# Routing the first 27 chunks of an attention and expert kernel in three groups of nine, in seven pieces, behind the value products

## The chip, the cores and the metric

The kernel runs on one core of a Trainium2 chip. The metric is device time in microseconds (us). The core has TensorE (PE, and PEld for its weight loads), VectorE (DVE), ScalarE (ACT), GpSimd (POOL) and SyncE (SP, which issues most DMAs). Each engine works through its own instructions in program order and waits on semaphores for the others.

## The reference

A windowed causal attention over 8 batches, 8 heads, 576 rows and 64 columns a head, whose output of 4608 tokens by 512 columns goes into a mixture of 8 experts; each token goes to the one expert with the largest logit.

```python
scores = scale * np.matmul(q, k.transpose(0, 1, 3, 2))
mask = (rel >= 0) & (rel < window)                     # window = 128
scores = np.where(mask, scores + bias[None], -1000000000.0)
scores = scores - np.max(scores, axis=-1, keepdims=True)
attn = np.exp(scores)
attn = attn / (np.sum(attn, axis=-1, keepdims=True) + 1e-09)
x = np.matmul(attn, v)                                 # to (4608, 512)
logits = x @ w_gate
expert_idx = np.argmax(logits, axis=1)
for e in range(E):
    mask = expert_idx == e
    h = np.maximum(x[mask] @ w1[e], 0.0)
    out[mask] = gate_w[mask, None] * (h @ w2[e])
```

## The kernel before

The tokens are worked through in 36 chunks of 128 rows. Chunk `ch` is spread over the steps from `4*ch` on, and the work of several chunks is interleaved: a function `step(s)` issues, for step `s`, whatever the table `LAGS` has due there. Up to step 151 (`HAND = 152`) every engine keeps exactly this order. The steps of a chunk are four, and a step's number modulo 4 tells what it issues:

- **0**: the first scores of a chunk (the heads' first half: TensorE L129 and L138 into `s_ps`), the first transposes of the chunk before (L168, `pe` into `t_ps`, copied by ScalarE to `pT`, L170), and the weighing of the new scores: on VectorE a masked copy (L147 or L152) and the maximum `nmax` (L155), on ScalarE four exponentials (L159).
- **1**: `rows` of an older chunk: the row products (L206, into the bank `r_ps`), then on VectorE the reciprocal (L203), the scaling `x_sb` from `r_ps` (L211) and the logits `lg` (L1145); then the second transposes (L168).
- **2**: the second scores and their weighing, as in step 0.
- **3**: the value products of an older chunk (L196, 32 matmuls for most chunks, 16 for the first chunk of a batch; one chunk in nine, which holds the last 64 rows of two batches, has them in two halves).

There are two `s_ps` banks, one `t_ps` and one `r_ps`. A new `r_ps` can be written once everything that touched the old one is done.

**Routing.** When the logits of a group of chunks are there, `route` finds each token's expert and its place in that expert's list. It is a generator: at each `yield` it stops, and `step` resumes it at the end of a later step. The groups are in `GROUPS` as (first chunk, number of chunks G). Its pieces before are five: (1) from `mx` (L404) to `prev` (L417), on VectorE, with one exponential `ex` on ScalarE; (2) the rank products on TensorE (L421, L422, L425: G+1 matmuls) into spare columns of the current `r_ps`, then on VectorE `pick` (L427), which reads them, and eight short instructions up to `t` (L438; a ninth, `s_cnt`, where a group ends with chunk 26), with the gates' DMAs on SP's queue (L496); (3) `p`, `lp` (L448, 128 columns a chunk), `c`, `big`; (4) `c`, `c`, `eq` (L458, 48 columns a chunk) and the two `rr` (L462); (5) the index products on TensorE (L468, 2G matmuls) into the spare columns of the then current `r_ps`, and their sum into `base` on VectorE (L470). For the group that ends with chunk 26, piece 3 also holds `shift_late` (one matmul L478 and five VectorE instructions from L480 on), whose result the chunks from 27 on need.

A group without an entry in `PACE` has one piece in each step of one kind (`s % 4`); a group with an entry (by its first chunk) has its pieces in the steps that the entry lists. The group (30, 5) is routed from step 149 on and finished in `route_last`, which also routes chunk 35. At step 134 the first lists are read (`e_idx`), and rows are gathered for the first expert. From step 58 to 113 each chunk also has ScalarE and GpSimd split a half of a weight tile (`wh` L924, `wl` L929).

After the attention the experts' two layers run, weights streamed, with TensorE as the engine that everything else feeds.

Of the kernel before, what the change touches and what calls it, by code (L numbers as in the profile page):

```python
# [10 lines left out]
F32 = mybir.dt.float32  # L11
F32R = mybir.dt.float32r
BF16 = mybir.dt.bfloat16
# [8 lines left out]
N, DM, E, F = B * S, H * D, 8, 1024  # L22
# [14 lines left out]
def attention(ctx, tc, st, qT, kT, v, c1, cb, iw, load_c2, chunk_done, chunks, begun):  # L37
# [48 lines left out]
    def warm_up(n):  # L86
        w_ps = ps_x.tile([128, 512], F32, name="x_ps")
        for _ in range(n):
            keep(tc, nc.tensor.matmul(out=w_ps, lhsT=warm[:, 0:128], rhs=warm, start=True, stop=True))

    def early(op):
        bank = ps_s.tile([128, 2, 2, 256], F32, name="s_ps")[:, 0] if op not in "zg" else None
        st["early"][0](op, bank if bank is None else bank.rearrange("p a b -> p (a b)"))
# [124 lines left out]
    for ch, subs in enumerate(chunks):  # L218
        for b, i in subs:
            k = (b, i // 4)  # L220
# [48 lines left out]
    def step(s):  # L269
        st["step"] = s  # L270
        if s == 0:
            begun(0)
        if s == 12:
            begun(1)
        for f, b, m in ahead.get(s, ()):
            f(b, m)
        for k, ch in sorted(plan.get(s, ()), key=lambda x: (1.5 if x[0] == 9 else x[0], x[1])):
            do(k, ch)
        if s < len(WU) - 1:
            warm_up(WU[s + 1])  # L280
        for k in list(st["stages"]):
            if k[1] <= s and (s in PACE[k[2]] if k[2] in PACE else s % 4 == 2):
                k[1] = s + 1
                if next(k[0], k) is k:
                    st["stages"].remove(k)
        n, i = divmod(s - FETCH, 8)
        if 0 <= n < 7 and i in (0, 1, 4, 5):
            (st["round"], st["rest_of"])[i % 4](n, i // 4)
        if (s - FETCH + 12) % 8 == 0 and 0 <= (s - FETCH + 12) // 8 < 8:
            st["load"]((s - FETCH + 12) // 8)  # L290
        if s in EP:
            early(EP[s])

    with tc.manual_schedule(engines=HANDS(nc)):
        HELD[0] = True
        for s in range(HAND):
            step(s)
        HELD[0] = False
    for s in range(HAND, max(plan) + 1):
        step(s)  # L300
# [29 lines left out]
TT = 6  # L330
# [5 lines left out]
LW = (0, 0, 0, 0)  # L336
FREE_T = 146
WU = (9, 1, 1, 1, 1, 1, 2, 2, 2, 2, 2, 1, 0)
PACE = {21: (122, 126, 130, 132, 134), 27: (138, 142, 144, 146, 148), 30: (149, 150)}
GROUPS = ((0, 5), (5, 5), (10, 5), (15, 6), (21, 6), (27, 3), (30, 5), (35, 1))  # L340
EARLY = 256
LATE = 27
NE = 7
# [51 lines left out]
def route(tc, st, lg, c0, G, groups):  # L395
    nc = tc.nc
    rp = st["rp"]
# [3 lines left out]
    sc3 = [128, G, E * TT]  # L401
    sp3 = [128, G, 128]
# [31 lines left out]
    s = st["rank"][:, c0:c0 + G]  # L434
# [8 lines left out]
    if c0 + G == LATE:  # L443
        shift_late(tc, st, cnt)
    p = rp.tile([128, G], F32, name="p")
    nc.vector.scalar_tensor_tensor(out=p, in0=t, scalar=-128.0, in1=s, op0=ALU.mult, op1=ALU.add)
    lp = rp.tile(sp3, BF16, name="lp")
    nc.vector.tensor_tensor(out=lp, in0=st["i128"].unsqueeze(1).to_broadcast(sp3),  # L448
                            in1=p.unsqueeze(2).to_broadcast(sp3), op=ALU.is_equal)
    c = rp.tile([128, G], F32, name="c")  # L450
    nc.vector.tensor_scalar(out=c, in0=mk, scalar1=-float(TT), scalar2=float(TT * E), op0=ALU.mult, op1=ALU.add)
    big = rp.tile([128, G], F32, name="big")
    nc.vector.tensor_scalar(out=big, in0=s, scalar1=128 * TT - 0.5, scalar2=1000.0, op0=ALU.is_ge, op1=ALU.mult)
    yield
    nc.vector.tensor_tensor(out=c, in0=c, in1=t, op=ALU.add)
    nc.vector.tensor_tensor(out=c, in0=c, in1=big, op=ALU.add)
    eq = rp.tile(sc3, F32, name="eq")
    nc.vector.tensor_tensor(out=eq, in0=st["i128"][:, 0:E * TT].unsqueeze(1).to_broadcast(sc3),  # L458
                            in1=c.unsqueeze(2).to_broadcast(sc3), op=ALU.is_equal)
    rr = rp.tile([128, G, 2, E * TT], BF16, name="rr")  # L460
    for k, n in enumerate(("tokh", "tokl")):
        nc.vector.tensor_tensor(out=rr[:, :, k, :], in0=eq,  # L462
                                in1=st[n][:, c0:c0 + G].unsqueeze(2).to_broadcast(sc3), op=ALU.mult)
    yield
# [34 lines left out]
def route_last(tc, st, lg, ch, groups):  # L499
    nc = tc.nc  # L500
    rp = st["rp"]
# [19 lines left out]
    nc.tensor.matmul(out=rank, lhsT=tri[:, 0, :], rhs=oh, start=True, stop=False)  # L521
    nc.tensor.matmul(out=rank, lhsT=tri[:, 1, :], rhs=prev, start=False, stop=True)
    for r in st["rest"]:
        next(r)
        next(r)
    st["warm"](1)
    rr = rp.tile([128, 2, E], BF16, name="l_rr", bufs=1)
    for k, n in enumerate(("tokh", "tokl")):
# [2 lines left out]
    s = st["rank"][:, ch:ch + 1]  # L531
# [8 lines left out]
    for t in range(t0, TT):  # L540
        lp = rp.tile([128, 128], BF16, name=f"l_lp{t}", bufs=1)
# [577 lines left out]
def attn_moe_kernel(ctx, tc, qT, kT, v, c1, cb, c2, iw, w12, out):  # L1119
# [9 lines left out]
    with ExitStack() as actx:  # L1129
# [9 lines left out]
        def done(ch, subs, x_sb):  # L1139
            c0, G = next((c, n) for c, n in GROUPS if c <= ch < c + n)  # L1140
            g = ch - c0
# [12 lines left out]
            if g == G - 1:  # L1154
# [16 lines left out]
                else:  # L1171
                    r = route(tc, st, lg, c0, G, groups)
                    st["stages"].append([r, st["step"] + (c0 not in PACE), c0])

# [46 lines left out]
```

## Time and profile before

| | us |
|---|---|
| median of 3 runs | 672.38 (671.96 to 673.99) |
| the profiled execution | 670.84, with a span of 669.1 |
| TensorE busy | 645.0 |
| VectorE busy | 397.8 |
| ScalarE busy | 315.3 |
| GpSimd busy | 311.7 |

The span runs from the first to the last instruction; the 1.7 us between it and the execution's own time lie around it. Busy times are sums over the span; waits are told by the instruction that came last before the waiting one could start. The attention with its routing takes roughly the first 235 us of the span, the experts the rest. TensorE's granted clock is 1.00 in nearly the whole span.

### The profile page before, as it was taken

To read this page: it belongs to the slowest core of one execution; us is meant where nothing else is said; L and a number is where in the kernel's file an instruction comes from. 1 tells how busy PE (TensorE), PEld (TensorE's weight loads), DVE (VectorE), ACT (ScalarE), POOL (GpSimd) and SP (SyncE) were. 2 spreads that over 40 slices of the span, in tenths; PEclk is the share of its full clock that TensorE was granted. 3 is DMA by queue.
4 is the path that set the end of the run, shared out by engine and by line. 5 is a ranking of instruction groups with operands and counts; after the bars stand their busy time and mean duration, and the time that the engine had idled before them with its cause. 6 is when DMAs were issued, how large, how long until landed. Compare 5 with 4: busy or idle time off the path is not lost.

```text
span 669.1 us, 15750 instructions
## 1 busy us (share of the span) xinstructions
PE 645.0 (96%) x5985; PEld 546.8 (82%) x5985; DVE 397.8 (59%) x984; ACT 315.3 (47%) x957; POOL 311.7 (47%) x420
## 2 busy tenths in 40 slices
PE   8899999999999989999999999999999999999995
PEld 3587787887787878889888989898898989888884
DVE  3468878887888877554564465455456455456411
ACT  3677787888787521442343334233333333333311
POOL 2556466786764504016525742860762560471202
PEclk9999999999999999999999999999999999999998
DMA  8676797795862416428344433533542533454201
GB/s 316 200 199 175 182 235 174 241 260 151 259 160 65 97 50 190 126 111 273 106 146 151 132 100 110 163 101 97 168 125 84 183 105 82 157 145 110 91 1 58
DMA packets 57488, 98.43 MB, mean 147 GB/s; under 512 B 11701, under 2 KB 31413, under 8 KB 56514
## 3 DMA queue, kind: packets, MB, share of 16 engines
q1 hardware_dynamic: 48994, 77.38, 39.4%
q0 software_dynamic: 8416, 20.02, 10.5%
q8 instruction: 48, 0.79, 0.5%
q14 instruction: 30, 0.25, 0.1%
HBM read 78.40 MB, written 18.98 MB: 146 GB/s over the span
## 4 chain that ended last, share of the span: by engine, by line
PE 51%; issue 9%; POOL 4%; DVE 1%; DMA 1%; ACT 1%; POOLq 0%; ACTq 0%
PE y_ps L820 24%; PE l_ps L637 24%; POOL xg L617 2%; POOL out L808 1%; PE s_ps L637 1%; PE x_ps L598 1%; PE x_ps L196 1%; PE y_ps L780 1%; DMA xg<-xd,idx 0%; PE r_ps L206 0%; DMA xd<-x_sb 0%; DVE x_sb L211 0%; PE x_ps L780 0%; ACT pe L159 0%; POOLq L872 0%
## 5 line engine op out<-in xcount | busy, mean ns | idle before, releaser
L640 ACT ACTIVATE hh<-l_ps 128x336 fp32r<-128x336 f32 (+7 forms) x104 | 46.4, 447 | 203.4 <-PE l_ps L637 203.1
L641 DVE SCALAR_TENSOR_TENSOR hl<-l_ps,hh 128x336 fp32r<-128x336 f32 (+7 forms) x104 | 52.1, 502 | 150.2 <-ACT hh L640 150.1
L617 POOL DMA_INDIRECT xg<-xd,od_idx x112 | 118.1, 1054 | 36.9 <-issue 36.2
L159 ACT ACTIVATE pe<-s_ps,nmax 128x128 f32<-128x128 f32 x288 | 102.2, 371 | 48.9 <-DVE nmax L155 39.5
L820 PE MATMUL y_ps<-wh,hh 128*128 128x512 f32 (+5 forms) x280 | 110.9, 396 | 0.0
L820 PE MATMUL y_ps<-wh,hl 128*128 128x512 f32 (+5 forms) x280 | 110.4, 394 | 0.0
L820 PE MATMUL y_ps<-wl,hh 128*128 128x512 f32 (+5 forms) x280 | 110.3, 394 | 0.0
L808 POOL DMA_INDIRECT out<-y,od_pidx x33 | 34.8, 1055 | 149.3 <-ACT y L826 143.1
L912 DVE TENSOR_TENSOR wl<-w_raw,wh 128x512 fp32r<-128x512 f32 x114 | 73.8, 689 | 32.9 <-ACT wh L908 30.8
L637 PE MATMUL l_ps<-xh,wh 128*128 128x304 f32 (+9 forms) x416 | 81.7, 318 | 0.0
L637 PE MATMUL l_ps<-xh,wl 128*128 128x304 f32 (+9 forms) x416 | 81.0, 317 | 0.0
L637 PE MATMUL l_ps<-xl,wh 128*128 128x304 f32 (+9 forms) x416 | 80.8, 316 | 0.0
L637 PEld LDWEIGHTS l_ps<-xh,wh 128*128 128x128 f32 x416 | 68.1, 189 | 8.4 <-issue 1.2
L637 PEld LDWEIGHTS l_ps<-xh,wl 128*128 128x128 f32 x416 | 66.4, 189 | 1.9
L637 PEld LDWEIGHTS l_ps<-xl,wh 128*128 128x128 f32 x416 | 66.3, 189 | 1.7
L196 PE MATMUL x_ps<-pT,v_sb 128*64 128x128 f32 (+2 forms) x1152 | 66.3, 265 | 0.1
L196 PEld LDWEIGHTS x_ps<-pT,v_sb 128*64 128x64 f32 (+1 forms) x1152 | 57.0, 137 | 7.9 <-issue 2.8
L820 PEld LDWEIGHTS y_ps<-wh,hl 128*128 128x128 f32 (+5 forms) x280 | 51.4, 184 | 13.6
L908 ACT CAST wh<-w_raw 128x1024 fp32r<-128x1024 f32 x57 | 59.5, 1044 | 5.5 <-DMA w_raw<-w 5.5
L820 PEld LDWEIGHTS y_ps<-wl,hh 128*128 128x128 f32 (+5 forms) x280 | 51.6, 184 | 11.3
L159 ACT ACTIVATION_READ_ACCUMULATOR pe<-s_ps,nmax 128x1 f32 x288 | 60.2, 209 | 0.0
L138 PE MATMUL s_ps<-k_sb,q_sb 64*64 64x192 f32 (+2 forms) x1152 | 58.3, 311 | 1.9 <-DMA k_sb<-kT 1.9
(211 smaller groups left out, 972.6 us busy)
## 6 DMA issues: line engine op xcount, KB each, us to landing
w_raw<-w SPq DMA_DIRECT2D x64, 512.0 KB, 3.9
q_sb<-qT SPq DMA_DIRECT2D x40, 256.0 KB, 6.4
xd<-x_sb SPq DMA_DIRECT2D x32, 258.0 KB, 4.8
v_sb<-v SPq DMA_DIRECT2D x32, 256.0 KB, 5.2
k_sb<-kT SPq DMA_DIRECT2D x7, 1152.0 KB, 8.5
w_n<-w SPq DMA_DIRECT2D x4, 1024.0 KB, 8.0
xg<-xd,od_idx POOLq DMA_INDIRECT x112, 2.9
xd<-x_sb SPq DMA_DIRECT2D x8, 129.0 KB, 4.8
```

The source lines that it names most:

```text
L138: nc.tensor.matmul(out=s_ps[halves(a), c, n, x0:x1], lhsT=blocks["q", b, m][h, 2 * g + n, qs], rhs=batch[b][h, 2 * g + n, k0:k0 + x1 - x0] ...
L159: nc.scalar.activation(out=pe[:, h, :], in_=s_ps[:, c, n, lo:lo + 128], func=AF.Exp, bias=nmax[:, 2 * c + n:2 * c + n + 1], scale=1.0, acc ...
L196: nc.tensor.matmul(out=x_ps[64 * c:64 * c + 64, p, q], lhsT=blocks["v", b, m - 1 + kb][0:kk, D * h:D * h + D], rhs=pT[0:kk, kb, h, q], sta ...
L598: nc.tensor.transpose(out=x_ps[:, d, :], in_=g[:, SUB * d:SUB * d + 128], identity=st["ident"])
L617: ins = tc.nc.gpsimd.indirect_dma_start(out=g[:, s], out_offset=None, in_=parts, in_offset=bass.IndirectOffsetOnAxis(ap=idx[:, s], axis=0),)
L637: nc.tensor.matmul(out=ps, lhsT=a[:, 128 * d:128 * d + 128], rhs=b[:, d], start=(k == 0), stop=(k == 11))
L640: nc.scalar.activation(out=hh, in_=ps, func=AF.Relu)
L641: nc.vector.scalar_tensor_tensor(out=hl, in0=ps, scalar=0.0, in1=hh.bitcast(F32), op0=ALU.max, op1=ALU.subtract)
L808: ins = nc.gpsimd.indirect_dma_start(**kw).ins
L820: nc.tensor.matmul(out=ys[t][0:n], lhsT=a[:, tl], rhs=b[:, 512:1024], start=(f == 0 and k == 0), stop=(f == 7 and k == 2))
L908: keep(tc, nc.scalar.copy(out=wh, in_=raw))
L912: keep(tc, eng.tensor_tensor(out=wl[:, sl], in0=raw[:, sl], in1=wh.bitcast(F32)[:, sl], op=ALU.subtract))
```

## The change

The first 27 chunks go in three groups of nine in place of groups of 5, 5, 5, 6 and 6. Pieces 3 and 4 are cut anew, into five: (3) `p`, `lp`; (4) `c`, `big`, `c`, `c`, `eq`; (5) the first `rr`; (6) the second `rr`; (7) the index products, as piece 5 was. Groups without a `PACE` entry resume at the end of steps with `s % 4 == 3`, so behind the value products, in place of `s % 4 == 2`, behind the second scores. The `PACE` entries of the groups that start at chunk 18 (before: 21) and 27 have seven steps. `lp`, `eq` and `rr` have one buffer in place of two. `route_last` resumes the group (30, 5) four times in place of two, which reaches the same place.

```diff
-            if k[1] <= s and (s in PACE[k[2]] if k[2] in PACE else s % 4 == 2):
+            if k[1] <= s and (s in PACE[k[2]] if k[2] in PACE else s % 4 == 3):
...
-PACE = {21: (122, 126, 130, 132, 134), 27: (138, 142, 144, 146, 148), 30: (149, 150)}
-GROUPS = ((0, 5), (5, 5), (10, 5), (15, 6), (21, 6), (27, 3), (30, 5), (35, 1))
+PACE = {18: (122, 124, 126, 128, 130, 132, 134), 27: (138, 140, 142, 144, 145, 146, 148), 30: (149, 150)}
+GROUPS = ((0, 9), (9, 9), (18, 9), (27, 3), (30, 5), (35, 1))
...
-    lp = rp.tile(sp3, BF16, name="lp")
+    lp = rp.tile(sp3, BF16, name="lp", bufs=1)
     nc.vector.tensor_tensor(out=lp, in0=st["i128"].unsqueeze(1).to_broadcast(sp3),
                             in1=p.unsqueeze(2).to_broadcast(sp3), op=ALU.is_equal)
+    yield
     c = rp.tile([128, G], F32, name="c")
...
     nc.vector.tensor_scalar(out=big, in0=s, scalar1=128 * TT - 0.5, scalar2=1000.0, op0=ALU.is_ge, op1=ALU.mult)
-    yield
     nc.vector.tensor_tensor(out=c, in0=c, in1=t, op=ALU.add)
     nc.vector.tensor_tensor(out=c, in0=c, in1=big, op=ALU.add)
-    eq = rp.tile(sc3, F32, name="eq")
+    eq = rp.tile(sc3, F32, name="eq", bufs=1)
...
-    rr = rp.tile([128, G, 2, E * TT], BF16, name="rr")
+    rr = rp.tile([128, G, 2, E * TT], BF16, name="rr", bufs=1)
     for k, n in enumerate(("tokh", "tokl")):
+        yield
         nc.vector.tensor_tensor(out=rr[:, :, k, :], in0=eq,
...
     for r in st["rest"]:
-        next(r)
-        next(r)
+        for _ in range(4):
+            next(r)
```

How the instructions move is told by their order on each engine. **First place**, TensorE, the rank products of the first group (`tri` and `oh`), before: they stand behind the second scores (L138) and ahead of the value products (L196).

```order
L138 MATMUL s_ps<-k_sb,q_sb 64x128 x2
L421 LDWEIGHTS tri
L421 MATMUL r_ps<-oh,tri 128x40
L422 LDWEIGHTS tri
L422 MATMUL r_ps<-prev,tri 128x40
L425 LDWEIGHTS tri
L425 MATMUL r_ps<-oh,tri 128x32
L425 LDWEIGHTS tri
L425 MATMUL r_ps<-oh,tri 128x24
```

The same of the change, TensorE, four chunks later in the program:

```order
L138 MATMUL s_ps<-k_sb,q_sb 64x192 x8
L196 MATMUL x_ps<-pT,v_sb 64x128 x16
L421 LDWEIGHTS tri
L421 MATMUL r_ps<-oh,tri 128x72
L422 LDWEIGHTS tri
L422 MATMUL r_ps<-prev,tri 128x72
```

They stand behind the value products now; the index products of the first two groups move in the same way.

**Second place**, VectorE around steps 122 to 125, before: behind the first piece of the group that ends with chunk 26 (its last instruction is `prev`) come the weighing of step 124 and the `rows` of step 125.

```order
L417 CAST prev<-run 128x8
L152 COPY_PREDICATED s_ps<-c_sb,s_ps 128x4x64
L155 TENSOR_REDUCE nmax<-s_ps 128x4
L203 RECIPROCAL rinv<-rsum 128x8
L211 TENSOR_TENSOR x_sb<-r_ps,rinv 128x4x16
L211 TENSOR_TENSOR x_sb<-r_ps,rinv 128x4x128
L1145 TENSOR_REDUCE lg<-x_sb 128x8
```

The same of the change:

```order
L417 CAST prev<-run 128x8
L152 COPY_PREDICATED s_ps<-c_sb,s_ps 128x4x64
L155 TENSOR_REDUCE nmax<-s_ps 128x4
L427 TENSOR_TENSOR pick<-r_ps,oh 128x72
L429 TENSOR_REDUCE gate<-ex 128x9
```

The second piece (`pick` and nine more) stands between the weighing of step 124 and the `rows` of step 125 now; before, it stood behind the weighing of step 126.

**Third place**, TensorE around steps 140 and 141 (group 27, three chunks), before: scores, first transposes, row products, second transposes, and the next scores.

```order
L138 MATMUL s_ps<-k_sb,q_sb 64x192 x8
L168 MATMUL t_ps<-c_sb,pe 128x128 x4
L206 MATMUL r_ps<-iw_sb,xT 128x144 x4
L168 MATMUL t_ps<-c_sb,pe 128x128 x4
L129 LDWEIGHTS cb_sb
```

The same of the change:

```order
L138 MATMUL s_ps<-k_sb,q_sb 64x192 x8
L168 MATMUL t_ps<-c_sb,pe 128x128 x4
L421 LDWEIGHTS tri
L421 MATMUL r_ps<-oh,tri 128x24
L422 LDWEIGHTS tri
L422 MATMUL r_ps<-prev,tri 128x24
L425 LDWEIGHTS tri
L425 MATMUL r_ps<-oh,tri 128x16
L425 LDWEIGHTS tri
L425 MATMUL r_ps<-oh,tri 128x8
L206 MATMUL r_ps<-iw_sb,xT 128x144 x4
L168 MATMUL t_ps<-c_sb,pe 128x128 x4
```

The rank products stand between the first transposes and the row products now, there and, with 72 columns, at step 124; before, they stood behind the second scores of steps 142 and 126. The row products write a new `r_ps`, so they come after `pick` has read the old one.

## Rows read from the trace of the kernel before

**Rows 1.** From the page: the span, and busy time (share of the span) and instructions of each engine.

```profile
span 669.1 us, 15750 instructions
...
PE 645.0 (96%) x5985; PEld 546.8 (82%) x5985; DVE 397.8 (59%) x984; ACT 315.3 (47%) x957; POOL 311.7 (47%) x420
```

**Rows 2.** Busy time of each engine in three stretches: the chunks in which the first four groups are routed, the next eight chunks or so, and the experts. Columns: the stretch, its length, busy us (and instructions) by engine, granted clock, share of the DMA engines, GB/s.

```profile
41.90:187.40 145.50, 139.04 (x2376) 114.72 (x2379) 118.04 (x292) 113.85 (x474) 94.54 (x150) 1.00 0.77 206
187.40:224.80 37.40, 35.63 (x619) 29.64 (x618) 32.58 (x92) 27.65 (x119) 21.19 (x38) 1.00 0.54 126
264.00:660.00 396.00, 396.00 (x2210) 346.39 (x2210) 198.01 (x429) 138.44 (x234) 163.84 (x179) 1.00 0.40 123
```

**Rows 3.** The waits of TensorE between 24 and 224 us: who waited for whom, us in total, times, longest.

```profile
PE t_ps L168 <- ACT pT L170: 4.9, 10, 0.7
PE r_ps L468 <- DVE x_sb L211: 3.1, 4, 1.2
PE r_ps L421 <- DVE x_sb L211: 0.4, 1, 0.4
```

**Rows 4.** Instructions in order of time where the first group's index products run (here and below: start us, length us, engine, line, operation, tiles; in brackets the idle time before and what ended it).

```profile
80.49 0.19 DVE L203 RECIPROCAL rinv<-rsum 128x8 f32<-128x8 f32 x1
...
80.77 0.82 DVE L211 TENSOR_TENSOR x_sb<-r_ps,rinv 128x64 f32<-128x64 f32 x2
...
81.64 0.41 PE L468 MATMUL r_ps<-rr,lp 128*128 128x48 bf16 x10 [0.88 <-DVE x_sb L211]
...
81.68 0.68 DVE L152 COPY_PREDICATED s_ps<-c_sb,s_ps 128x512 f32<-128x512 uint32 x1
...
81.98 1.97 PE L196 MATMUL x_ps<-pT,v_sb 128*64 128x128 f32 x32
```

**Rows 5.** Instructions in order of time, from a maximum to the second transposes of a chunk whose value products come in halves.

```profile
101.28 0.69 DVE L155 TENSOR_REDUCE nmax<-s_ps 128x4 f32<-128x512 f32 x1
...
103.45 0.62 ACT L924 CAST wh<-w_raw 128x512 fp32r<-128x512 f32 x1
...
103.96 0.60 ACT L170 COPY pT<-t_ps 128x512 f32<-128x512 f32 x1
...
104.61 0.65 PE L168 MATMUL t_ps<-c_sb,pe 128*128 128x128 f32 x4 [0.55 <-ACT pT L170]
```

**Rows 6.** TensorE in order of time around the second group's rank products, which had no wait.

```profile
93.12 0.18 PE L421 MATMUL r_ps<-oh,tri 128*128 128x40 bf16 x1
...
93.34 1.97 PE L196 MATMUL x_ps<-pT,v_sb 128*64 128x128 f32 x32
95.24 0.41 PE L129 MATMUL s_ps<-cb_sb 64*64 64x256 bf16 x8
...
97.70 0.60 PE L168 MATMUL t_ps<-c_sb,pe 128*128 128x128 f32 x4
```

**Rows 7.** VectorE in order of time at the same place: a weighing, the second piece of the group, the next weighing.

```profile
93.21 0.70 DVE L147 COPY_PREDICATED s_ps<-c_sb 128x512 f32<-128x512 uint32 x1
...
94.55 0.19 DVE L427 TENSOR_TENSOR pick<-r_ps,oh 128x40 f32<-128x40 f32 x1
...
96.44 0.70 DVE L152 COPY_PREDICATED s_ps<-c_sb,s_ps 128x512 f32<-128x512 uint32 x1
```

**Rows 8.** VectorE in order of time where the groups that start at chunks 21 and 27 are routed: end of the first piece and the weighing of step 124, the second piece's ends, the third piece with `shift_late`, and end of the first piece and the weighing of step 140.

```profile
194.85 0.16 DVE L417 CAST prev<-run 128x8 bf16<-128x8 f32 x1
...
195.37 0.69 DVE L155 TENSOR_REDUCE nmax<-s_ps 128x4 f32<-128x512 f32 x1
...
198.73 0.20 DVE L427 TENSOR_TENSOR pick<-r_ps,oh 128x48 f32<-128x48 f32 x1
...
200.72 0.69 DVE L147 COPY_PREDICATED s_ps<-c_sb 128x512 f32<-128x512 uint32 x1
...
204.58 0.15 DVE L480 TENSOR_SCALAR s_short<-r_ps 128x8 f32<-128x8 f32 x1
...
206.41 0.96 DVE L448 TENSOR_TENSOR lp<-c_sb,p 128x768 bf16<-128x768 f32 x1
207.28 0.17 DVE L451 TENSOR_SCALAR c<-mk 128x6 f32<-128x6 f32 x1
...
220.08 0.16 DVE L417 CAST prev<-run 128x8 bf16<-128x8 f32 x1
...
220.87 0.69 DVE L155 TENSOR_REDUCE nmax<-s_ps 128x4 f32<-128x512 f32 x1
```

**Rows 9.** TensorE in order of time at the same places: the row products of step 125, the second transposes of step 133, the index products and the value products behind them, the row products and second transposes of step 141, and the value products of step 143.

```profile
194.99 1.15 PE L206 MATMUL r_ps<-iw_sb,xT 128*128 128x144 f32 x8
...
207.68 0.60 PE L168 MATMUL t_ps<-c_sb,pe 128*128 128x128 f32 x4
...
211.55 0.46 PE L468 MATMUL r_ps<-rr,lp 128*128 128x48 bf16 x12 [1.17 <-DVE x_sb L211]
211.94 1.18 PE L196 MATMUL x_ps<-pT,v_sb 128*64 128x64 f32 x28
...
219.54 1.15 PE L206 MATMUL r_ps<-iw_sb,xT 128*128 128x144 f32 x8
220.91 0.65 PE L168 MATMUL t_ps<-c_sb,pe 128*128 128x128 f32 x4 [0.22 <-ACT pT L170]
...
222.81 1.97 PE L196 MATMUL x_ps<-pT,v_sb 128*64 128x128 f32 x32
```

## The prediction

> **What bounds the kernel now.** I read the page first, then busy time by stretch, the waits of TensorE, and the order of time where routing pieces run. TensorE is busy for 645.0 of 669.1 us [rows 1]. Among the experts it is busy in all of 396.00 us, and in the stretch in which the first four groups are routed in 139.04 of 145.50 [rows 2]. So whatever the attention gains or loses on TensorE reaches the end one for one, and nothing in the experts' part is touched. In the attention the most that a better routing can win is what TensorE idles there, 6.5 us, and some tenths that the modelled ends of matmuls hide; the next stretch idles 1.8 of 37.4. VectorE is busy 118.04 of 145.50 us (81%): late in places, not the bound.
>
> The waits say what the idle time is [rows 3]: 3.1 us at the index products and 0.4 at the rank products, both for `x_sb`, and 4.9 at the transposes, for ScalarE's copy to `pT`. The first kind is routing's own: its products go into the spare columns of `r_ps`, and wait until VectorE has scaled `x_sb` out of that bank. In [rows 4] TensorE stands 0.88 us for this, since VectorE, held by the piece before, starts its reciprocal only at 80.49 and is through with `x_sb` at 81.6.
>
> The second kind is mostly not routing's. In [rows 5] the maximum ends at 101.97; the four exponentials, the weight half (103.45), and the copy to `pT` (103.96 to 104.56) follow on ScalarE, and the transposes start at 104.61. That chain takes 2.64 us from the maximum, 2.1 where no weight half lies in it, and stalls TensorE where the value products between are short. That stall stays, whatever VectorE does.
>
> **The change, part by part**, against the profiled execution's own 670.84 us (1.5 under the median of 672.38).
>
> *Gains in the first four groups, which become two.* The waits for `x_sb` at their index products are 3.1 less the 1.17 of the fifth group [rows 3, 9], so 1.9; behind 1.9 us of value products `x_sb` is long scaled. The 0.4 at the rank products goes likewise. TensorE's own routing time: five chunks take 0.22 for the rank products (93.12 to 93.34) [rows 6] and 0.34 for the index products (81.64 to 81.98) [rows 4], so some 2.3 for four groups; from their 6 and 10 matmuls at 0.03 to 0.04 each I take 0.35 and 0.55 for nine chunks, 1.8 for two groups, and save 0.5. Of the waits of the transposes I credit 0.7: those in chunks whose exponentials had a routing piece ahead. Together **3.5**. About 45 VectorE instructions and three gate DMAs fall away; both are covered, VectorE's by its idle 19%, and cost or win nothing beyond this.
>
> *A loss in the same two groups.* The second piece begins with `pick`, which reads the rank products. Before, these ran ahead of the value products, while VectorE weighed; `pick` found them done, and the piece ran from 94.55 to 96.44 beside the value products of 93.34 to 95.24 [rows 6, 7]. Behind the value products they end 1.9 + 0.35 us after the scores, a weighing takes 1.34 (93.21 to 94.55), so VectorE stands for 0.9 us and is busy with the piece (1.9, about 2.0 for nine chunks) while TensorE already makes the next scores (1.0). The next weighing starts some 1.2 us behind its scores. The next chunk is the first of a batch, whose short scores leave no room, so its second weighing is still 1.1 behind. Queued behind it are the exponentials, the copy to `pT`, and so the second transposes. In [rows 6, 7] these come at 97.70 without a wait; the maximum before them ends at 94.55 + 0.08, and 2.64 later would be 97.27, 0.2 of room once the rank products have moved away. So about 0.9 is lost, once in each group. The first piece's `ex` on ScalarE adds 0.3 in the second. **2.1.**
>
> *Group 18 to 26, paced by hand.* Its second piece is at step 124, between the first transposes and the row products. The row products need the old `r_ps` free, so `pick` done. VectorE, before: `prev` ends at 195.01 and the maximum at 196.06 [rows 8]. Five instructions on 72 columns in place of 48 add 0.1; `pick` takes 0.2; so the row products start at 196.4, not at 194.99 [rows 9]: 1.4 late. From there VectorE has no pause. The second piece takes 2.0 (198.73 to 200.72) and ends at 198.2. `rows` takes 1.2 (80.49 to 81.68) [rows 4], a weighing of the narrow kind 1.1, so 200.5. The third piece took 2.7 (204.58 to 207.28) and `lp` grows from 0.96 at 768 columns to 1.37 at 1152 (0.15 fixed, as the smallest rows show): 3.1, so 203.6. Weighing 1.35; fourth piece 1.2 (four instructions at 0.15, `eq` at 432 columns by the slope of `lp`); `rows` 1.2; weighing 1.35: the maximum of step 130 ends at 208.7. The transposes of step 133 follow 2.1 to 2.2 later, at 210.9, not at 207.68 [rows 9]. From those to the index products it was 3.87 with 1.1 of waiting; that wait is gone now (`x_sb` is scaled during the second scores), and the index products take 0.55. The value products behind them start at 210.9 + 2.75 + 0.55 = 214.2, not at 211.94. **2.3 lost**, the removed wait counted.
>
> *Group 27.* The same at step 140: `prev` ends at 220.24, the maximum at 221.56 [rows 8], `pick` at 221.65, so the row products start at 221.7 in place of 219.54 [rows 9]. The transposes behind them had a wait of 0.4 of their own, which this covers: 222.7 in place of 220.91. From there to the value products it was 1.9, of which the rank products' 0.25 have moved: 224.3 in place of 222.81. **1.5 lost.** The new pieces at 144 to 146 lie where the old ones lay.
>
> Edits at nothing: the single buffers of `lp`, `eq` and `rr` (their last reader, the index products, is several steps back; if it were not, VectorE would wait out the rest of a group's 0.55 us); the pieces 5 and 6, 0.5 us each, which fit VectorE's pauses; the group (30, 5).
>
> The Trainium skill, "Perfetto Trace Analysis", section "Optimizing Scalar/DVE Operations", says two things that pull against each other here: grouping into larger operations improves throughput if the engine is saturated, and if it is not, but causes bubbles on others, breaking instructions up may let work finish sooner. By the first, nine chunks at once are a gain, the second speaks against them; VectorE at 81% [rows 2] is under the second, so the larger `lp` and the longer pieces weigh more than the instructions saved. No run here shows it yet.
>
> **Sum:** -3.5 + 2.1 + 2.3 + 1.5 = +2.4 us: 673.2 on the profiled execution's scale, 674.8 on the median's.
>
> **Rivals.**
> 1. *About as before.* Same steps, smaller sizes: if the second pieces of the first two groups cost nothing (0 to 2.1), or the backlog of group 18 drains earlier and only its 1.4 remains. Then +0 to +1.5, about 673.2. For it: the lateness is a difference of long sums, each off by tenths. Against it: the two late row products alone are 2.9.
> 2. *Faster.* The transposes' waits are after all routing's lateness on VectorE, which two light groups leave out. They are 4.9 us in [rows 3] and up to 6 with the modelled ends; if more than 5.1 went in place of my 0.7, the change would pass -2 us. At 6 it is -2.9: 669.5. For it: half of these waits lie in chunks with pieces. Against it: [rows 5], where the chain behind the maximum, with no piece in it, is enough.
> 3. *VectorE is the bound.* Then what counts is its time saved: two groups' fixed shares, some 22 instructions of 0.15 each, 3.3 a group, so 6.6 and 665.8. Against it: 27 us of idle VectorE in the stretch [rows 2].
> 4. *Clearly slower.* Each late maximum finds short value products behind it and the lateness adds up: 2 us more in the first two groups and 1 more in group 18: 677.8.
>
> **How the numbers follow.** What a measurement of this kernel can tell from no change is about 0.3%, 2.0 us. Chances: forecast (over +2, up to +4.5) 0.43; about as before 0.38; faster 0.11 and VectorE as the bound 0.02; clearly slower 0.06. So slower 0.49, same 0.38, faster 0.13. Bounds: the waits of the transposes give 0 to 6, the two new lags 0 to 4, group 18 1.4 to 3.3, group 27 1 to 2. With 1 in 10 left out at each end: 670.2 to 677.6. The likeliest case's own range is 674.4 to 676.9.
>
> **What would show it.** The waits for `x_sb` at index and rank products gone in the first two groups, right if under 0.3 in all. A new wait of the row products for `pick`, about 0.9 to 1.4 (beside 0.6 for `oh` and `prev` at step 140), at two places. A wait of the second transposes for `pT` of 1.5 to 2 at step 133, and of 0.5 to 1.3 two steps behind each `pick` of the first two groups. VectorE without a pause from step 122 to 132. Wrong would be the forecast if the row products did not wait, if the value products of step 135 came less than 1 us later, measured from step 122, or if the transposes' waits shrank as a whole.

## The result and the profile after

The changed kernel takes **676.47 us** (median of 19 executions, 672.53 to 679.67); the kernel before, beside it, 672.30. The ratio is **1.0056**, 95% interval [1.0043, 1.0069]: slower by 0.6%. It was profiled in an execution of 676.87 us with a span of 675.1. From the two `rr` on its lines are one higher (L463 is L462 of before, L469 is L468). TensorE's waits up to the end of the attention, as in [rows 3]:

```profile
PE t_ps L168 <- ACT pT L170: 7.7, 11, 1.7
PE r_ps L206 <- DVE pick L427: 2.0, 2, 1.2
PE r_ps L421 <- DVE oh L415: 1.5, 1, 1.5
PE s_ps L129 <- ACT pe L159: 0.9, 1, 0.9
PE r_ps L206 <- DVE x_sb L211: 0.2, 1, 0.2
```

The 3.5 us of waits for `x_sb` at index and rank products in [rows 3] are gone; 0.2 is left, at row products. In their place stand two waits of the row products for `pick`, one of rank products for `oh`, one of scores for `pe`, and longer waits of the transposes. TensorE in order of time at the hand-paced groups:

```profile
192.79 1.25 PE L206 MATMUL r_ps<-iw_sb,xT 128*128 128x144 f32 x8 [0.82 <-DVE pick L427]
...
206.95 0.66 PE L168 MATMUL t_ps<-c_sb,pe 128*128 128x128 f32 x4 [1.66 <-ACT pT L170]
...
219.88 0.17 PE L421 MATMUL r_ps<-oh,tri 128*128 128x24 bf16 x1 [1.52 <-DVE oh L415]
...
221.37 2.29 PE L206 MATMUL r_ps<-iw_sb,xT 128*128 128x144 f32 x8 [1.20 <-DVE pick L427]
...
226.29 2.36 PE L196 MATMUL x_ps<-pT,v_sb 128*64 128x128 f32 x32
```

The waits for `pick` (0.82 and 1.20 us) and for `pT` (1.66) are those forecast; the one for `oh` was forecast as 0.6 and is 1.52. The fourth row shows something else too: eight row products take 2.29 us, 1.15 in [rows 9]. Busy time in windows of 1 us (the eighth column, behind the five engines, is the granted clock):

```profile
219.00:220.00 1.00, 0.12 (x3) 0.12 (x3) 0.90 (x6) 1.00 (x7) 0.14 (x1) 1.00 0.92 190
220.00:221.00 1.00, 0.18 (x4) 0.08 (x2) 0.97 (x2) 1.00 (x4) 0.52 (x2) 0.66 0.31 103
...
226.00:227.00 1.00, 1.00 (x16) 0.71 (x10) 0.56 (x1) 0.00 (x0) 0.55 (x1) 0.50 0.89 190
227.00:228.00 1.00, 1.00 (x20) 1.00 (x20) 0.93 (x4) 0.04 (x1) 0.00 (x0) 0.93 0.14 30
```

After TensorE had stood for 1.52 us, and while it stood again for `pick`, its clock fell to half (1.2 GHz of 2.4) and stayed there for 6.8 us (the windows left out are at 0.50).

To see where the time went I take the ends of the last value products of chunks 3, 28, 32 and 35 from TensorE's rows in order of time. Chunks 4 to 28 hold the routing of the first 18 chunks, 29 to 32 and 33 to 35 that of the hand-paced groups; the rest is the experts. One profile of each kernel, in us; "half clock" is how long TensorE's clock stood at half within chunks 29 to 35:

| kernel | 4-28 | 29-32 | 33-35 | rest | half clock | ratio of the times [95%] |
|---|---|---|---|---|---|---|
| before | 151.72 | 24.50 | 16.64 | 434.35 | 0 | 1 |
| before, again (e0) | 151.85 | 24.51 | 18.07 | 435.66 | 0 | |
| **changed** | 150.62 | 26.30 | 22.46 | 436.32 | 6.8 | 1.0056 [1.0043, 1.0069] |
| e1, 27 at 142 | 150.61 | 26.30 | 18.49 | 435.39 | 0 | 1.0012 [1.0001, 1.0022] |
| e2, 18 at 126 | 150.57 | 27.73 | 18.18 | 436.36 | 3.4 | 1.0036 [1.0023, 1.0049] |
| e3, both | 150.56 | 26.09 | 18.15 | 436.19 | 0 | 1.0031 [1.0013, 1.0049] |
| e4, filled waits | 150.56 | 26.27 | 20.12 | 435.67 | 0 | 1.0041 [1.0028, 1.0054] |
| e5, place alone | 149.09 | 24.51 | 18.07 | 435.74 | 0 | **0.9954 [0.9938, 0.9971]** |
| e6, groups alone | 148.23 | 27.49 | 16.97 | 435.60 | 3.4 | 0.9978 [0.9965, 0.9991] |
| e7, sevens | 148.64 | 25.46 | 18.25 | 434.38 | 0 | 0.9972 [0.9962, 0.9982] |
| e8, fives mixed | 153.85 | 24.50 | 18.09 | 436.51 | 0 | 1.0028 [1.0014, 1.0042] |
| e9, nines mixed | 152.85 | 28.76 | 16.95 | 435.99 | 6.8 | 1.0069 [1.0042, 1.0097] |
| e10, sevens mixed | 150.45 | 24.99 | 18.28 | 435.41 | 0 | 1.0000 [0.9986, 1.0014] |
| e11, `pick` third | 148.29 | 28.72 | 16.94 | 434.23 | 6.8 | 0.9991 [0.9978, 1.0005] |

Five kernels with the same first two groups (the changed one, e1 to e4) agree within 0.06 us in the first column, and the two profiles of before within 0.13, so it can be read to one or two tenths. What is missing to the span is the part up to the end of chunk 3, which no edit touches: it lies between 39.0 and 41.9 us in these profiles (39.45 in the changed kernel, 41.90 and 40.29 in the two of before), so spans of single profiles are not to be compared to better than some 3 us. One of e5's six executions took 1048.71 us at a mean granted clock of 0.557 and is left out of its ratio.

### The profile page after: what moved, and what is told of

The parts are those of the page before. It is cut to its first block, busy times and chain, and to the rows that moved or that the text cites. A ratio compares the mean times of both kernels' runs of the same rounds, so it can differ in the third digit from the quotient of the medians.

```text
span 675.1 us, 15669 instructions
## 1 busy us (share of the span) xinstructions
PE 646.4 (96%) x5981; PEld 547.2 (81%) x5983; DVE 389.6 (58%) x934; ACT 314.5 (47%) x955; POOL 311.4 (46%) x420
## 4 chain that ended last, share of the span: by engine, by line
PE 61%; DVE 1%; ACT 0%; issue 0%; POOLq 0%; POOL 0%; ACTq 0%
PE y_ps L821 30%; PE l_ps L638 29%; PE x_ps L599 1%; PE y_ps L781 1%; PE x_ps L781 0%; PE s_ps L638 0%; DVE e_hl L642 0%; ACT wh L909 0%; POOLq L986 0%; DVE lp L448 0%; PE l_ps L610 0%; DVE y L829 0%; DVE wl L913 0%; ACT e_hh L641 0%; DVE hl L642 0%
## 5 line engine op out<-in xcount | busy, mean ns | idle before, releaser
L618 POOL DMA_INDIRECT xg<-xd,od_idx x112 | 114.5, 1022 | 37.4 <-issue 36.8
L196 PE MATMUL x_ps<-pT,v_sb 128*64 128x128 f32 (+2 forms) x1152 | 66.7, 266 | 0.1
L196 PEld LDWEIGHTS x_ps<-pT,v_sb 128*64 128x64 f32 (+1 forms) x1152 | 57.4, 137 | 10.1 <-issue 3.5
L152 DVE COPY_PREDICATED s_ps<-c_sb,s_ps 128x512 f32<-128x512 uint32 (+1 forms) x56 | 36.8, 656 | 43.8 <-PE s_ps L138 40.8
```

Source lines behind the costliest of these rows:

```text
L152: nc.vector.copy_predicated(out=s4[:, :, 0:w], mask=(tail_sb if tail else fold_sb)[:, 0:w].unsqueeze(1).to_broadcast(sh), data=s4[:, :, 12 ...
L196: nc.tensor.matmul(out=x_ps[64 * c:64 * c + 64, p, q], lhsT=blocks["v", b, m - 1 + kb][0:kk, D * h:D * h + D], rhs=pT[0:kk, kb, h, q], sta ...
L618: ins = tc.nc.gpsimd.indirect_dma_start(out=g[:, s], out_offset=None, in_=parts, in_offset=bass.IndirectOffsetOnAxis(ap=idx[:, s], axis=0),)
```

## The experiments

Theory: the first two groups gain by fewer waits and lose at `pick`; the paced groups lose where `pick` now stands (steps 124, 140); and the clock falls because TensorE stands there. Rivals: the larger pieces lose wherever they stand; the clock and the late weighings come and go by themselves.

**e1, group 27's second piece back at step 142.**

```diff
-27: (138, 140, 142, 144, 145, 146, 148)
+27: (138, 142, 143, 144, 145, 146, 148)
```

> The changed kernel with one number back: the second piece of group 27 stands at step 142 again, behind the second scores, not at step 140. Between the ends of chunks 32 and 35 the changed kernel takes 22.46 us, the kernel before 16.64. Theory (the piece at step 140 makes TensorE stand for oh and for pick, and TensorE's granted clock falls behind that): both waits and the fall go, the stretch is back at 16.7 to 18, and the whole takes 4 to 5.5 us less than the changed kernel, about 671.5 to 672.5. Rival (the late weighing of step 138 and the clock come from something else, the gather that GpSimd issues there or chance): only the 1.5 us that I had forecast go, the clock still falls between 220 and 227 us, about 675.

672.67 us, 3.8 under the changed kernel. Both waits and the fall are gone, the stretch 4.0 shorter. So the piece at step 140 costs about 4 us with what follows it, where I had 1.5. The stretch is still 1.85 above the first profile of before; e0 tells why.

**e2 and e3, group 18's second piece two steps later, alone and with e1.**

```diff
-18: (122, 124, 126, 128, 130, 132, 134)
+18: (122, 126, 130, 131, 132, 133, 134)
```

> The changed kernel with the second piece of group 18 two steps later: its pieces are at 122, 126, 130, 131, 132, 133 and 134 in place of 122 to 134 by twos. Theory (row products wait for pick at step 124, VectorE is late from there to step 133): the stretch from chunk 28's end to chunk 32's, 26.30 us in the changed kernel and 24.50 before, falls to 24.5 to 25.0, and the time to about 674.8; the fall of the clock behind step 140 stays. Rival (it is the larger pieces that make VectorE late, wherever they stand): the stretch stays within 0.5 of 26.3, since four pieces now follow each other from 130 to 133, and the time at about 676.5.

> The changed kernel with both numbers moved: group 18's second piece behind step 126, group 27's behind step 142. Theory (what the two hand-paced groups lose is due to the place of their second pieces, 1.8 and 5.8 us): both stretches are back at about 24.6 and 16.8 us, what is left is the gain of the first two groups (1.1 us net), about 670.5 to 671.5, which is under the kernel before. Rival (the losses are those of nine chunks at once and of longer pieces): over 673.5.

The theory falls here. e3, with no half clock there, takes 26.09 us in chunks 29 to 32 where the changed kernel takes 26.30. `pick` no longer holds the row products, but the pieces behind it are crowded, and e3's waits of TensorE show the bill at the index products:

```profile
PE r_ps L469 <- DVE x_sb L211: 1.9, 1, 1.9
...
PE r_ps L469 <- DVE rr L463: 0.5, 1, 0.5
```

2.4 us there for the 0.82 and 1.66 above: the loss moves with the pieces. e3 takes 673.22 us, between the two forecasts and 0.55 over e1, where the intervals overlap. e2 takes 674.40, near the theory's 674.8, but not for the theory's reason: its stretch of chunks 29 to 32 is longer (27.73), and the gain lies in chunks 33 to 35. It still has group 27 at step 140, and in its profile no half clock there: 18.18 us. Its rank and row products of group 27:

```profile
220.42 0.17 PE L421 MATMUL r_ps<-oh,tri 128*128 128x24 bf16 x1
...
221.91 1.25 PE L206 MATMUL r_ps<-iw_sb,xT 128*128 128x144 f32 x8 [1.20 <-DVE pick L427]
```

The wait for `pick` is the same 1.20 us, but there is none for `oh`. So the 1.52 us of the changed kernel do not come from the place alone; e0 shows what else is in them.

**e4, TensorE kept busy at step 140.** It repeats the first transposes four times and group 27's rank products six times.

```diff
+        for _ in range(4 if st["step"] == 140 else 1):
             for j in range(4):
                 nc.tensor.transpose(out=t_ps[:, j, :], ...)
...
+    for _ in range(6 if c0 == 27 else 1):
         nc.tensor.matmul(out=rank, lhsT=tri[:, 0, :], ...)
```

> The changed kernel in which TensorE repeats work at step 140 where it stood: the first transposes four times, and the rank products of group 27 six times, with the same values; it only fills the 1.5 us in which it waited for oh and the 1.2 us in which it waited for pick. Theory (the clock falls behind these waits because TensorE stood): the granted clock stays at 1.00 from 220 to 230 us, and the time is 2 to 3 us under the changed kernel's, about 674. Rival (the clock falls there for another reason, or by chance in some executions): the clock falls as before, and the time is that of the changed kernel or up to 0.5 us more, 676.5 to 677.

Its TensorE at the two waits, and its windows:

```profile
221.79 0.17 PE L423 MATMUL r_ps<-oh,tri 128*128 128x24 bf16 x1 [0.19 <-DVE oh L416]
...
223.29 1.25 PE L207 MATMUL r_ps<-iw_sb,xT 128*128 128x144 f32 x8 [0.69 <-DVE pick L430]
```

```profile
220.00:225.00 5.00, 4.11 (x55) 3.68 (x57) 4.66 (x19) 4.08 (x19) 2.46 (x5) 1.00 0.45 105
225.00:230.00 5.00, 4.87 (x72) 4.17 (x72) 2.97 (x8) 3.02 (x12) 1.47 (x3) 1.00 0.30 56
```

Work that computes nothing new keeps the clock full, and chunks 33 to 35 take 20.12 us for 22.46. Four of its five executions have a mean granted clock of 0.998 or 0.999; of the changed kernel's 19, three have 0.997 or more (672.53, 673.84 and 673.96 us, its three fastest). The median gains 1.0 us (675.49), less than the 2 to 3 expected, and the intervals of the two ratios overlap, so the whole time alone shows no gain. Up to the row products the fill shows no cost in the two profiles: they start 4.98 us behind the end of chunk 32, and 5.00 in the changed kernel. Why more of the 2.3 us does not reach the median is open.

**e0, the kernel before once more,** profiled beside e5 to e7.

> The kernel before, unchanged, profiled once more beside the three below. In every kernel with the change so far VectorE began the weighing of step 138 or 139 late (1.6 us behind its scores in three of five) and the part behind the last value products took 1.0 to 1.9 us more than the 434.34 us in the first profile of before; in those traces ScalarE and VectorE also start some instructions 0.5 to 5 us behind the matmuls they wait for. Theory (this belongs to the changed programs): none of it here, the last part within 0.3 us of 434.3, span about 669 to 670.5. Rival (it comes and goes between executions or chips): it shows here too, and the last part takes 435 us or more.

The rival holds. Chunks 33 to 35 take 18.07 us and the rest 435.66, 1.4 and 1.3 more than in the first profile, with nothing changed. VectorE in the changed kernel, then in this one, at the same weighing:

```profile
217.00 0.69 DVE L152 COPY_PREDICATED s_ps<-c_sb,s_ps 128x512 f32<-128x512 uint32 x1 [1.89 <-remote]
```

```profile
217.17 0.69 DVE L152 COPY_PREDICATED s_ps<-c_sb,s_ps 128x512 f32<-128x512 uint32 x1 [1.77 <-PE s_ps L138]
```

Both begin 1.6 us or so after the scores' last matmul ended by the profile; in the first profile of before and in e2 it is 0.15. Why the release comes late is open; it does not need the change, and nine of the fourteen profiles have it. It is also what the wait for `oh` is made of: with the late weighing the changed kernel's rank products at step 140 stand for 1.52 us, without it, in e2, not at all. Before, and in e1, these rank products come two steps later and do not wait. Against this profile the changed kernel (spans 675.15 and 670.38) differs by -0.8 up to chunk 3, **-1.2, +1.8, +4.4** in the three stretches and +0.7 behind them.

**e5, the place alone:** groups of five and six as before, unpaced pieces behind the value products.

```diff
-... if k[2] in PACE else s % 4 == 2):
+... if k[2] in PACE else s % 4 == 3):
```

> The kernel before with one part of the change: in the groups that no table paces, pieces are issued at the fourth step of a chunk (behind its value products), not at the third; groups, pieces and the two tables stay. Theory (behind the value products x_sb is ready, but pick comes 0.9 us late): the waits for x_sb at index and rank products in the first four groups go (2.3 us), each group's second piece makes the second transposes two steps behind it late by 0.7 to 1.2 us, four times; from chunk 3's end to chunk 28's 152 to 153.5 in place of 151.72; time 672.5 to 674. Rival (the place alone brings the gain of the first two groups, which was 1.1 us): 150 to 151, and 671 to 672.

The theory falls, and this one line beats both kernels: 668.22 us beside 671.07. Its waits of TensorE, and its second pieces on VectorE:

```profile
PE t_ps L168 <- ACT pT L170: 5.8, 10, 1.3
PE r_ps L468 <- DVE x_sb L211: 1.2, 1, 1.2
```

```profile
62.36 0.20 DVE L427 TENSOR_TENSOR pick<-r_ps,oh 128x40 f32<-128x40 f32 x1 [0.31 <-PE r_ps L425]
...
91.11 0.20 DVE L427 TENSOR_TENSOR pick<-r_ps,oh 128x40 f32<-128x40 f32 x1 [0.63 <-PE r_ps L425]
...
121.89 0.20 DVE L427 TENSOR_TENSOR pick<-r_ps,oh 128x40 f32<-128x40 f32 x1 [0.60 <-PE r_ps L425]
...
158.04 0.20 DVE L427 TENSOR_TENSOR pick<-r_ps,oh 128x48 f32<-128x48 f32 x1
```

Of the `x_sb` waits at index products only the fifth group's is left; 2.6 us are gained, a little more than the 2.3 of the waits. `pick` stands for 0.3 to 0.6 us in three of the four groups, and little of it reaches TensorE.

**e6, the groups alone:** nines in seven pieces at the third step as before; paced groups as in e3.

```diff
-... if k[2] in PACE else s % 4 == 3):
+... if k[2] in PACE else s % 4 == 2):
```

> Groups of nine with seven pieces, as in the changed kernel, but pieces at the third step of a chunk as before, and the second pieces of groups 18 and 27 at steps 126 and 142; beside the kernel with both numbers moved it differs by the place of the first two groups' pieces alone. Theory (fewer groups save own time and waits, the place behind the value products costs 0.9 a group at pick, but saves the x_sb waits): each of the two groups waits about 0.9 for x_sb at its index products and does not wait at pick; from chunk 3's end to chunk 28's 149.5 to 151, against 150.5 with pieces at the fourth step; the time within 1 us of that kernel's 673.2. Rival (the place is what brings the gain): over 152.

669.82 us beside 671.07, and in chunks 4 to 28 148.23 us: 3.5 under before and **2.3 under the same groups at the fourth step** (150.56). `pick` starts without a wait:

```profile
85.04 0.22 DVE L427 TENSOR_TENSOR pick<-r_ps,oh 128x72 f32<-128x72 f32 x1
...
139.07 0.22 DVE L427 TENSOR_TENSOR pick<-r_ps,oh 128x72 f32<-128x72 f32 x1
```

I had expected 0.9 us a group for `x_sb` here, and 149.5 us at least. There is no such wait. The routing on VectorE in the chunk ahead of the first group's index products, before and then in e6:

```profile
76.90 0.58 DVE L455 TENSOR_TENSOR c<-c,t 128x5 f32<-128x5 f32 x1
...
78.51 0.73 DVE L462 TENSOR_TENSOR rr<-eq,c_sb 128x240 bf16<-128x240 f32 x2
```

```profile
109.61 1.05 DVE L463 TENSOR_TENSOR rr<-eq,c_sb 128x432 bf16<-128x432 f32 x1
...
113.60 0.63 PE L469 MATMUL r_ps<-rr,lp 128*128 128x48 bf16 x18
```

Before, the piece ahead took 2.3 us (`c`, `c`, `eq` and both `rr`) and made the weighing and `x_sb` behind it late; now it is one `rr` of 1.05 us, and the index products start without a wait. So it seems that cutting the pieces cures the same wait that the place cures. This is read from the order of time: no run has the seven pieces with the old groups. The place alone (e5) gains 2.6 us in chunks 4 to 28 and the groups with their pieces alone (e6) 3.5, but both together 1.1: the place adds nothing to the groups but the loss at `pick`.

**e7, three groups of seven,** 21 to 26 as one group in seven pieces, all at the fourth step.

```diff
-GROUPS = ((0, 9), (9, 9), (18, 9), (27, 3), (30, 5), (35, 1))
+GROUPS = ((0, 7), (7, 7), (14, 7), (21, 6), (27, 3), (30, 5), (35, 1))
```

> The first 21 chunks in three groups of seven, chunks 21 to 26 as one group as before, with the new pieces and places: group 21 at steps 122, 126, 130 to 134, group 27 with its second piece at 142. Theory (what the change loses is lost in the large group 18 and at step 140; smaller paced groups give VectorE its pauses back): from chunk 28's end to chunk 32's 24.5 to 25.2 in place of 26.3, chunks 33 to 35 in 16.7 to 17.5, the first stretch 150.5 to 151.5; 670.5 to 672, under the kernel before or level with it. Rival (the new pieces cost wherever they stand): 673 or more.

669.01 us beside 671.07: faster, and by more than forecast. The parts came out otherwise: chunks 4 to 28 under the forecast (148.64), chunks 29 to 32 and 33 to 35 over it (25.46 and 18.25, the latter with the late weighing). With six chunks the paced stretch costs 1.0 over before, with nine 1.6 to 1.8 at full clock. Of the 1.0, 0.45 lies in chunk 29 (6.50 us for 6.05), where the index products of the third group of seven now fall (step 123); in e10 below they come four steps earlier, and the stretch costs 0.5 over before.

**e8 to e10, the second piece alone at the third step:** fives (on e5), nines (on e3) and sevens (on e7).

```diff
+            n = st.setdefault("pieces", {}).setdefault(k[2], 0)
-            if k[1] <= s and (... else s % 4 == 3):
+            if k[1] <= s and (... else s % 4 == (2 if n == 1 else 3)):
+                st["pieces"][k[2]] += 1
```

> Groups of nine, pieces at the fourth step of a chunk as in the changed kernel, but the second piece (rank products and pick) alone at the third step; second pieces of groups 18 and 27 at 126 and 142. From chunk 3's end to chunk 28's the kernel with all pieces at the fourth step took 150.56 us, that with all at the third 148.23. Theory (what the fourth step costs is pick alone, 0.96 us of waiting behind the value products and what follows it): 148.0 to 148.8 here. Rival (other pieces behind the value products cost as well, the long lp above all): 149.5 to 150.6. Behind chunk 28 as in the kernel with both numbers moved, 26 and 17 to 18 us, more by 1.5 where the clock falls.

> The kernel before with its own groups, pieces of the unpaced groups at the fourth step, but the second piece at the third. With all at the fourth step: 149.09 us from chunk 3's end to chunk 28's, pick waiting 0.31, 0.63, 0.60 and 0 us in the four groups. Theory (pick's wait costs there too): 148.0 to 148.8, a time 0.3 to 0.8 under that kernel's. Rival (with groups of five the wait for pick is hidden): 149.0 to 149.4, the same time; or the x_sb wait at the rank products comes back (0.4).

> Three groups of seven, chunks 21 to 26 as one paced group, all pieces at the fourth step but the second at the third; with all at the fourth step the stretch from chunk 3's end to chunk 28's took 148.64 us, and pick waited in one group of three (0.68 us). Theory (that wait costs 0.7 to 1.1): 147.6 to 148.2 and a time 0.5 to 1 under that kernel's. Rival (hidden): 148.4 to 148.9, the same time.

All three are worse by 1.8 to 4.8 us in chunks 4 to 28, which no theory had. The edit was at fault: the third piece became due one step behind the second, so two pieces met in one chunk. e9 in order of time, second group:

```profile
141.84 0.22 DVE L429 TENSOR_TENSOR pick<-r_ps,oh 128x72 f32<-128x72 f32 x1
...
144.11 1.27 POOL L932 TENSOR_TENSOR wl<-w_raw,wh 128x512 fp32r<-128x512 f32 x1 [0.30 <-ACT wh L927]
...
144.15 2.44 DVE L450 TENSOR_TENSOR lp<-c_sb,p 128x1152 bf16<-128x1152 f32 x1
...
150.04 0.41 PE L129 MATMUL s_ps<-cb_sb 64*64 64x256 bf16 x8 [1.93 <-ACT pe L159]
```

The routing holds VectorE from 141.84 to 146.6, and TensorE's scores wait 1.93 us. So they don't tell where `pick` should stand, and the three forecasts stay untested in chunks 4 to 28; the runs tell what two pieces in a row cost.

**e11, the same for nines, third piece a chunk later.**

```diff
-                k[1] = s + 1
+                k[1] = s + (4 if n == 1 and k[2] not in PACE else 1)
```

> As the nines with the second piece at the third step, but the third piece (the long lp) waits for the fourth step of the next chunk; before, it came in the step right behind the second, so that VectorE ran 4.9 us of routing in one stretch and the scores waited for it. Beside the kernel with both numbers moved (150.56 us from chunk 3's end to chunk 28's, all pieces at the fourth step) it moves the second pieces of the first two groups by one step, beside the kernel with nines at the third step (148.23) all other pieces. Theory (what the fourth step costs with groups of nine is the second piece alone, with its 0.96 us for pick): 148.0 to 148.9, both late weighings (7.05 and 8.40 us in chunks 13 and 22 where 6.32 and 6.77 would do) gone. Rival (it is a long piece beside GpSimd's work in chunk 22, wherever pick stands): chunk 22 stays over 8 and the stretch at 149.7 or more.

The theory holds: 148.29 us; chunks 13 and 22 take 6.34 and 6.78 (7.05 and 8.40 in the changed kernel). The second piece behind the value products is the whole loss of the first two groups. The time, 0.9991 of before, is no better: the gain of 3.4 goes into chunks 29 to 32, which take 28.72 us, 1.6 more for group 18 as in e3 and 2.6 more for 6.8 us of half clock.

## Why the prediction was right, and where it was not

The forecast was slower, 674.8 us in 670.2 to 677.6; it came out slower, 1.7 above. Three of the four terms held within about 0.5 us. The fourth, group 27, was too small by 3 to 4 in the profiles, since no step of the sum had the fall of the clock, which costs 2.3, and the wait for `oh` was taken too short. The medians differ by 4.2 us, the profile of the changed kernel by 6.0 and 4.8 from the two of before, so how near the whole came to the forecast is partly luck.

*Gain of the first groups, 3.5:* e6 gives 3.5, e11 3.4. The size held, the reason only in part: I put the `x_sb` waits down to the place, and in e6 they are gone without it.

*Loss at `pick` there, 2.1:* 150.62 less 148.23 is 2.4, and e11 shows that it is this piece. `pick` stood 0.96 us each time for 0.9 forecast; chunk 13 loses 0.7, chunk 22 1.6. But the sign that I had named, a wait of the second transposes two steps behind each `pick`, is not there: those transposes start without a wait, and the lateness reaches TensorE only some 6 to 10 us behind `pick` (0.51 us at the transposes of chunk 13, 0.89 and 0.89 at scores and transposes in chunk 22). In chunk 22 VectorE also ran beside GpSimd, which I had not seen. The changed kernel there, in order of time:

```profile
140.47 0.23 DVE L427 TENSOR_TENSOR pick<-r_ps,oh 128x72 f32<-128x72 f32 x1 [0.96 <-PE r_ps L425]
...
141.70 1.27 POOL L930 TENSOR_TENSOR wl<-w_raw,wh 128x512 fp32r<-128x512 f32 x1 [0.30 <-ACT wh L925]
...
141.81 1.18 DVE L437 TENSOR_SCALAR t<-rank 128x9 f32<-128x9 f32 x1
143.03 0.58 DVE L438 TENSOR_SCALAR t<-t 128x9 f32<-128x9 f32 x1
...
146.59 0.41 PE L129 MATMUL s_ps<-cb_sb 64*64 64x256 bf16 x8 [0.89 <-ACT pe L159]
...
150.11 0.66 PE L168 MATMUL t_ps<-c_sb,pe 128*128 128x128 f32 x4 [0.89 <-ACT pT L170]
```

`t`, nine elements wide, takes 1.18 us and ends at 142.99, when GpSimd's `wl` ends (142.97). In chunk 13 of the same trace, with no `wl` beside it, it takes 0.17. That the larger loss of chunk 22 comes from this is read from the order of time; no run takes `wl` away with `pick` in its place.

*Group 18, 2.3:* 1.8 measured, with the waits named (`pick` 0.82, second transposes 1.66 for 1.5 to 2) and VectorE without a pause. But the place of `pick` is not its cause, as I had it: e3 moved it and lost 1.6. In this stretch the larger group costs wherever its second piece stands: beside e3's 26.09 us, six chunks with the same steps and pieces take 24.99 (e10), so 1.1 goes with nine chunks in place of six and 0.5 with the new pieces and steps.

*Group 27, 1.5:* this is the mis-sized term, +4.4 to +5.8. The mechanism was right: e2, with the piece at step 140, the full clock there and no late weighing, takes 18.18 us, 1.5 over the 16.64 of before. To this come 2.3 for 6.8 us of half clock (22.46 less e4's 20.12), and the late weighing, 1.4 to 2.0, which before has in one profile of two. The two are tied: it is the late weighing that makes the rank products at step 140 wait 1.52 us for `oh`, where I had 0.6, and the clock fell where this wait and the one for `pick` came together, not with the latter alone (e2). I counted the waits as lost time and not what standing does to the clock.

*Experts, 0:* the rest differs by +0.7 from e0 and +2.0 from the first profile of before; before itself differs by 1.3. No loss is shown there.

*The two sentences of the Trainium skill on grouping* ("Perfetto Trace Analysis", section "Optimizing Scalar/DVE Operations"), read against the change: the one on breaking up instructions agrees with e6, where VectorE has room (81% in [rows 2]), nine chunks in shorter pieces gain 3.5 us, and the wait for `x_sb` is gone. The one on grouping for a saturated engine is not borne out: where VectorE has no pause (steps 122 to 132), nine chunks in place of six cost 1.1 us. What I had concluded from them, that the larger pieces weigh more than the instructions saved, came true in that stretch only.

## What to carry to other kernels

When two parts of a change cure the same wait, price them apart: here each alone gained 2.6 and 3.5 us in the first groups, and both together 1.1. Waits of TensorE that follow each other closely, as the 1.52 and 1.20 us here, are to be charged also with what its clock may do behind them. Moving a piece away from one wait is worth little where VectorE has no pause: the wait moves with it. Profile the old kernel twice before a difference of 1 to 2 us is laid on a change.

## What the runs showed of the hardware

**The clock.** Behind 1.52 us of standing, and early in the next 1.20, the granted clock fell to 1.2 GHz for 6.8 us, which cost 2.3 us; in chunks 29 to 32 of e9 and e11, beside e3, 6.8 us of it cost 2.7 and 2.6, and 3.4 us in e6 1.4 (27.49 less 26.09). It does not always follow. e6 and e3 wait alike at the index products (1.90 and 0.50 us); e6's windows, then e3's:

```profile
203.00:207.00 4.00, 2.09 (x57) 1.67 (x52) 3.81 (x11) 1.69 (x9) 0.00 (x0) 1.00 0.00 0
207.00:211.00 4.00, 3.51 (x67) 3.30 (x70) 2.02 (x5) 1.79 (x9) 1.43 (x3) 0.57 0.56 134
```

```profile
206.00:210.00 4.00, 2.09 (x57) 1.67 (x52) 3.81 (x11) 1.70 (x9) 0.00 (x0) 1.00 0.00 0
210.00:214.00 4.00, 3.51 (x81) 3.11 (x81) 2.70 (x6) 1.91 (x10) 1.43 (x3) 1.00 0.52 134
```

The same 4 us, 2.09 of them busy, are followed by 0.57 in the one and 1.00 in the other. The five kernels with nine chunks and the second piece of group 18 at step 126 (e2, e3, e6, e9, e11) have a fall there in four of five profiles, and a mean granted clock of 0.997 or more in 6 of 47 executions, where e1 has it in 9 of 11. The Trainium skill, "TensorE: Matmul & The Clock Gate", section "HAM oscillation — how this bites in real kernels", counts the throttled time times one half as lost. By it, as an estimate, 6.8 us would cost 3.4; the traces give 2.3 to 2.7. In the changed kernel TensorE stood for 1.1 of the 6.8 us anyway, which explains a part.

**VectorE beside GpSimd.** Started just behind GpSimd's `wl`, the short `t` above lasted until `wl` ended (1.18 us for 0.17), and `lp` of 1152 columns took 2.44 us in e9, for 1.36 where no `wl` ran beside it and the 1.37 that I had reckoned. The Trainium skill, "SBUF — State Buffer", section "SBUF: two separate sides", says that the two share one pair of ports as an exclusive lock: of a VectorE instruction in a two-port mode, or with two inputs in SBUF against a GpSimd one that reads SBUF, and a GpSimd instruction, the one that starts first has it for the whole instruction, and the other blocks. `lp` has two inputs in SBUF; in which mode `t` ran, no run here shows. The ends at 142.99 and 142.97 agree.
